# Attention and expert routing on one core: some preparation operations of the first three groups on GpSimd, and a new planned order

## The chip, the core and the metric

The kernel runs on one core of a Trainium2 chip. The metric is the time of one execution on the device in microseconds (us), with inputs and outputs in the chip's memory. Five engines run side by side, each through its own instruction list in order, and wait for one another by semaphores: TensorE (PE; its weight loads are shown as PEld), VectorE (DVE), ScalarE (ACT), GpSimd (POOL) and SyncE (SP, which here only issues transfers). An instruction that must wait holds back everything behind it in its engine's list.

## The reference, cut to what matters

```python
def _attn_ref(q, k, v, g_q, g_k):            # q, k, v: 8 batches, 12 heads, 448 tokens, 64 wide
    def rmsnorm(x, g):
        rms = np.sqrt(np.mean(x * x, axis=-1, keepdims=True) + 1e-06)
        return x / rms * g
    q_n, k_n = (rmsnorm(q, g_q), rmsnorm(k, g_k))
    scores = np.matmul(q_n, k_n.transpose(0, 1, 3, 2)) / np.sqrt(64)
    attn = np.exp(scores - np.max(scores, axis=-1, keepdims=True))
    attn = attn / (np.sum(attn, axis=-1, keepdims=True) + 1e-09)
    return np.matmul(attn, v)

def _moe_ref(x, w_gate, w1, w2):             # x: 3584 tokens, 768 wide; 8 experts, 448 tokens each
    order = np.argsort(-(x @ w_gate).flatten())
    ...                                      # greedy: best pair first, at most 448 tokens an expert
    for e in range(8):
        out[assigned == e] = np.maximum(x[assigned == e] @ w1[e], 0.0) @ w2[e]
```

The attention result, reordered to one row a token, is the input of the routing and of the experts.

## The kernel before, in words

**Three stages.** Attention fills the first 510 us or so of the span. Then the router finds the first expert's tokens, and the eight experts follow, one after another, with the router's later phases woven in between. The change touches attention alone; the experts' code and order are as before.

**How attention is tiled.** The 96 heads are taken in 24 groups of four. A group is two pairs of heads (a = 0 and a = 1 in the code). Queries and keys are prepared per group: ScalarE squares them (`square`), VectorE sums the squares (`sumsq`) and works out the inverse root in six small steps (`rsqrt`, L439 to L449), `norm` (L463) multiplies by it, `gain` (L488) multiplies the queries by the gains. To keep accuracy in float16 each of them is split in a high part (`hi_k`, `hi_q`: ScalarE casts, L493 and L498) and a low part (`lo_k` L525, `lo_q` L530: what the cast lost, a subtraction). High and low parts stand side by side in tiles `ks` and `qs` and are then transposed.

**From there to the output.** `max_score` (L657, L660) multiplies once for the row maxima, `max_reduce` (L671, VectorE) takes the maxima from the accumulation tiles `pm` and `psc`, `put_max` (L675) writes them to the tile `qm`, and they return as one more row of the query operand `q2`. `scores` (L688, L693) then makes the scores in `psc`, ScalarE exponentiates them (`exp`, L704, tile `e`), VectorE or GpSimd makes a low part of some of these (`split`, L720, tile `pl`), and `av` (L739 to L748) multiplies with the values into the accumulation tile `po`. ScalarE and VectorE prepare the values as well (`v_hi` L609, `v_lo` L612, `v_full` L626, `v_tail` L479).

**The first two groups** (g below `EARLY = 2`) are done a pair at a time, so that TensorE has work sooner, and are turned on TensorE (`turn_first`, L552) instead of by transfers. The copies out of that turn are one on VectorE (L558) and one on ScalarE (L564). Their row maxima return through a small TensorE product (`rows_first`, L571) and two copies (L578 on ScalarE, L580 on VectorE). From group 2 on, transposes and row copies are transfers in SP's list: L537 and L507 for `k` and `q`, L587 (`mt<-qm`) and L594 (`q<-mt`) for the row maxima, L801 and L803 (`xt<-xb`, `xt<-xm`) for the attention output of a finished batch (three groups) on its way to the router.

**Which engine does what.** `ENG` gives the engine of each such operation: D is VectorE, P GpSimd, A ScalarE, S a transfer. `FIRST` overrides it for the first groups. Rings limit how far work may run ahead: there is one buffer each for `kn` and `qn`, two for the raw loads (`raw`), three for `k1` and `k2`, two for `q2`.

**What sets the order.** The kernel writes out the whole order of attention itself. `plan` lists some thousands of tasks, each with a queue, an estimated duration (`US`), what it waits for and what it frees. Its place is a number worked out from the group or tile and an offset from the table `P`. `Plan.order` runs through time with a list of free engines and takes, on each engine, the ready task with the lowest place. That sequence is then issued as it stands, on every engine. So a change of one estimate, one engine or one number in `P` can change the order of all the rest. The chip does not see the plan's times, only its order.

**Router work inside attention.** `Router.early` (L1308 to L1348) ranks the experts for the first 21 columns of tokens. It is one task of the plan and gives twelve VectorE instructions in a row.

Of the kernel before, what the change touches and what calls it, by code (L numbers as in the profile page):

```python
# [32 lines left out]
OP = mybir.AluOpType  # L33
# [201 lines left out]
class Attention:  # L235
# [215 lines left out]
    def norm(self, g, i, a=None):  # L451
        name = ("qn", "kn")[i]
# [3 lines left out]
        if g < self.EARLY and i == 0:  # L456
            x = o
        r = self.stat(g, 1, a)[:, i]
        if a is None:
            r = r.rearrange("p (a u) -> p a u", a=2)[:, :, :, None]  # L460
        else:
            r = r[:, :, None]
        self.tt("norm" + "qk"[i], g)(o, x, r.to_broadcast(list(o.shape)), op=OP.mult)  # L463

    ENG = dict(lok="P", loq="P", dupk="S", dupq="S", normk="P", normq="P", gain="P", vfull="A", vtail="A")
    FIRST = (dict(gain="P", normq="P", normk="D", lok="D", loq="D"),
             dict(gain="P", normq="P", normk="P", lok="D", loq="P"), dict(gain="D"))
    TAIL = {}

    def engine(self, e, g):  # L470
        some = self.FIRST[g] if g < len(self.FIRST) else self.TAIL if g >= self.NG - 2 else {}
        return some.get(e, self.ENG[e])

    def tt(self, e, g):
        return (self.nc.gpsimd if self.engine(e, g) == "P" else self.nc.vector).tensor_tensor

# [6 lines left out]
    def gain(self, g, a=None):  # L483
        if g < self.EARLY and not a:
            self.T["qn", g] = self.w.tile([128, 14, 64], F32, name="qn", bufs=self.RINGS["qn"])
        t = self.T["qn", g][:, self.of(a)]
        x = self.raw(g, 0, a) if g < self.EARLY else t
        self.tt("gain", g)(t, x, self.gg[:, None, :].to_broadcast(list(t.shape)), op=OP.mult)  # L488

# [33 lines left out]
    def lo_k(self, g, a=None):  # L523
        t = self.T["ks1", g]
        self.tt("lok", g)(self.half(t, 0, a), self.paired(self.T["kn", g][:, self.of(a)], a), self.half(t, 64, a),  # L525
                          op=OP.subtract)

    def lo_q(self, g, a=None):
        t = self.T["qs1", g]
        self.tt("loq", g)(self.half(t, 64, a), self.paired(self.T["qn", g][:, self.of(a)], a), self.half(t, 0, a),  # L530
                          op=OP.subtract)
# [364 lines left out]
    def gate_sum(self, b):  # L896
# [4 lines left out]

    P = dict(av0=-0.67, av1=-0.55, av3=-233.82, dupk=-20.94, dupq=0.73, early=56.02, exp=-49.79, f01=-18.78,
             f01i=-213.71, f10=-7.45, f10i=-218.14, f11=-6.2, f11i=-725.64, gain=8.07, gate=10.58, gates=0.21,
             gg=-28.49, glast=151.09, gtail=-10.06, hik=40.19, hiq=51.14, lgg=-5.96, lok=10.05, loq=10.17,
             lqk=90.96, lqki=2.37, lqkr=-18.25, ltail=33.72, lv=-4.27, lvs=108.43, lwg=495.86, max=5.38,
             max01=0.85, max10=-25.87, max11=-265.16, ng0=-55.37, ng1=-1.86, normk=5.07, normq=-20, put=-26.68,
             r1=27.99, r2=-773.05, r3=2.11, r4=-73.44, r5=-759.09, r6=46.33, red=-406.74, rows=-84.95, split=-0.52,
             sq0=53.5, sq1=-491.03, ss0=153.72, ss1=175.4, t0=-496.84, t1=3, t2=-38.87, tg6=-1.43, trk1=-75.39,
             trm=-0.91, trq1=7.59, txt=-21.19, vfull=-20.55, vhi=14.06, vlo=44.07, vtail=-509.19, wg=60.43,
             xl=-22.58, xn=58.85, xn1=-39.78, xn2=0.1, xs=-173.13, xst=404.87, xstep=-91.79, xtd=-270.51,  # L910
             xturn=69.89)

# [216 lines left out]
    def plan_first(self, plan, g, a, t):  # L1129
# [11 lines left out]
        raw = [[("raw", 0, i, r) for r in (3 * a, 1, 2)] if g == 0 else [("raw", g, i)] for i in range(2)]  # L1141
        e = lambda name: self.engine(name, g)
        us = lambda name: {"D": d, "P": 0.95}[e(name)]
# [906 lines left out]
```

## Time and profile before

| | us |
|---|---|
| three runs | 1033.56, 1038.93, 1039.92 |
| median | 1038.93 |
| the profiled execution: its own time | 1024.11 |
| the profiled execution: span from first to last instruction | 1022.3 |

The profile shows one execution. Its own time is 1.8 us more than its span, and 14.8 us below the median of the three runs, so a sum that is made against its rows is a difference to be put on the median. Views give start and duration of an instruction in us, the engine, the line, the operation, the tiles as output<-inputs, the shapes, and in square brackets how long the engine sat idle before it and what released it. In a windows view each row is a stretch of time: its length, the busy time and the number of instructions of PE, PEld, DVE, ACT and POOL, the granted TensorE clock as a share of full speed, the transfer engines' share and GB/s.

### The profile page before, as it was taken

Reading aid. Unit: us, or ns where it says so; the run is one execution under the profiler, and the core shown is the slowest. Engines: PE = TensorE matmul, PEld = TensorE weight load, DVE = VectorE, ACT = ScalarE, POOL = GpSimd, SP = SyncE. Lnnn points to the kernel's source line nnn. Section 1 sums busy time; section 2 is a strip of 40 time slices with the busy share of each in tenths; the row PEclk is TensorE's granted clock in tenths of the full one; section 3 lists DMA queues with packets and bytes.
Section 4 is the critical chain, followed back from the end, with each engine's and each line's share of the span. In section 5 each row is a group of like instructions: output and inputs, shape, how many; then the busy total and the mean of one; then the engine's idle time right before and its main releaser. Section 6 shows DMA issues by size and latency. Waiting matters only on the chain. (4 is left out here: it accounts for less than half of the span.)

```text
span 1022.3 us, 23367 instructions
## 1 busy us (share of the span) xinstructions
PE 937.5 (92%) x9495; PEld 598.9 (59%) x9496; DVE 714.3 (70%) x1602; ACT 494.9 (48%) x816; POOL 403.9 (40%) x315
## 2 busy tenths in 40 slices
PE   2698999899898899989969999899999999999996
PEld 1366667667676576656746655555556565555554
DVE  7898878788688778898678777667676866425010
ACT  4767767577676757745514342333342423334111
POOL 3568686687577679653310110101111102020101
PEclk9999999899899999989959999999999999999998
DMA  5268798988879798766137463939493939654101
GB/s 148 70 141 195 151 221 173 184 203 178 199 167 202 181 227 203 146 157 115 45 120 236 158 198 122 265 107 288 134 247 110 300 103 229 234 137 150 39 3 52
DMA packets 275876, 167.01 MB, mean 163 GB/s; under 512 B 195896, under 2 KB 262968, under 8 KB 274744
## 3 DMA queue, kind: packets, MB, share of 16 engines
q1 hardware_dynamic: 251320, 138.70, 56.0%
q0 software_dynamic: 4608, 22.02, 6.4%
q10 hardware_dynamic: 19840, 4.79, 2.2%
q8 instruction: 74, 1.21, 0.5%
q14 instruction: 34, 0.28, 0.1%
HBM read 94.49 MB, written 22.02 MB: 114 GB/s over the span
## 5 line engine op out<-in xcount | busy, mean ns | idle before, releaser
L1835 PE MATMUL ph<-xt,w1h 128*128 128x448 f16 (+2 forms) x804 | 211.2, 344 | 0.8 <-ACT xt L1792 0.5
L739 PE MATMUL po<-v,e 128*128 128x65 f32 (+1 forms) x1392 | 185.8, 270 | 2.0 <-ACT e L704 1.9
L704 ACT ACTIVATE e<-psc 128x896 f32<-128x896 f32 x168 | 152.2, 917 | 65.1 <-PE psc L693 46.6
L739 PEld LDWEIGHTS po<-v,e 128*128 128x128 f32 (+1 forms) x1392 | 157.7, 181 | 28.2 <-issue 20.6
L1868 POOL DMA_INDIRECT out_dram<-y,idx x32 | 32.5, 1014 | 341.5 <-ACT y L1854 266.9
L693 PE MATMUL psc<-q,k 128*128 128x448 f16 x576 | 140.4, 364 | 24.9 <-DVE mx L671 10.2
L720 POOL TENSOR_TENSOR pl<-e 128x896 f16<-128x896 f32 x69 | 119.7, 1734 | 77.9 <-ACT e L704 60.0
L1835 PE MATMUL ph<-xt,w1l 128*128 128x448 f16 (+2 forms) x402 | 136.8, 344 | 0.0
L671 DVE TENSOR_REDUCE mx<-pm 128x2 f32<-128x896 f32 x96 | 104.5, 1088 | 38.1 <-PE pm L660 28.5
L1852 PE MATMUL py<-w2h,hl 128*128 128x384 f16 x384 | 125.5, 327 | 0.2 <-DVE hl L1827 0.2
L1852 PE MATMUL py<-w2h,hh 128*128 128x384 f16 x384 | 125.5, 327 | 0.2 <-ACT hh L1825 0.2
L1852 PE MATMUL py<-w2l,hh 128*128 128x384 f16 x384 | 125.5, 327 | 0.0
L1835 PEld LDWEIGHTS <-w1h 128*128 128x128 f16 x804 | 74.1, 97 | 61.9 <-issue 1.5
L1825 ACT ACTIVATE hh<-ph 128x448 f16<-128x448 f32 x64 | 34.7, 543 | 142.3 <-PE ph L1835 138.7
L744 PEld LDWEIGHTS <-e 128*128 128x128 bf16 (+1 forms) x840 | 88.1, 118 | 22.7 <-issue 18.0
L1852 PEld LDWEIGHTS <-hh 128*128 128x128 f16 x768 | 73.1, 97 | 45.8 <-ACT hh L1825 0.5
L1827 DVE SCALAR_TENSOR_TENSOR hl<-ph,hh 128x448 f16<-128x448 f32 x64 | 39.4, 621 | 78.2 <-ACT hh L1825 78.2
L1854 ACT ACTIVATE y<-py 128x384 f32<-128x384 f32 x48 | 23.5, 490 | 129.3 <-PE py L1852 102.7
L693 PEld LDWEIGHTS <-k 128*128 128x128 f16 x576 | 48.2, 99 | 63.1 <-issue 32.2
L671 DVE TENSOR_REDUCE mx<-psc 128x2 f32<-128x896 f32 x74 | 78.2, 1056 | 0.0
L746 PEld LDWEIGHTS <-e 128*128 128x128 bf16 (+1 forms) x840 | 73.0, 102 | 3.6 <-issue 0.4
L748 PEld LDWEIGHTS <-pl 128*128 128x128 f16 (+1 forms) x840 | 73.4, 102 | 2.1 <-POOL pl L720 2.0
(278 smaller groups left out, 2053.9 us busy)
## 6 DMA issues: line engine op xcount, KB each, us to landing
stage<-in_moe_w_dram SPq DMA_DIRECT2D x64, 768.0 KB
vraw<-in_v_dram SPq DMA_DIRECT2D x24, 384.0 KB
xd<-xb SPq DMA_DIRECT2D x8, 1152.0 KB
qkraw<-in_q_dram SPq DMA_DIRECT2D x23, 384.0 KB
qkraw<-in_k_dram SPq DMA_DIRECT2D x23, 384.0 KB
k<-k SPq DMA_DIRECT2D x44, 112.0 KB
q<-q SPq DMA_DIRECT2D x44, 112.0 KB
xd<-xm SPq DMA_DIRECT2D x16, 96.0 KB
```

The costliest lines, as they stand in the source:

```text
L671: self.nc.vector.tensor_reduce(m, p[:, :k, :448], axis=AX.X, op=OP.max)
L693: nc.tensor.matmul(p[:, i, :448], kt[:, a, 128 * u:128 * u + 128], qt[:, a, 448 * s:448 * s + 448], start=st, stop=not st)
L704: self.nc.scalar.activation(e, p[:, :, :448], AF.Exp, scale=scale)
L720: eng.tensor_tensor(l, self.T["e", d], self.T["ph", d], op=OP.subtract)
L739: nc.tensor.matmul(out, self.T["e", d][:, i, q0:q0 + m], self.v32[g % 2][:, self.by_group(self.WIDE, g).index(d % 7), i, :], start=first, ...
L744: nc.tensor.matmul(out, h[:, i, q0:q0 + m], vh, start=first, stop=False)
L746: nc.tensor.matmul(out[:, :64], h[:, i, q0:q0 + m], vl[:, :64], start=False, stop=False)
L748: nc.tensor.matmul(out, l[:, i, q0:q0 + m], vh, start=False, stop=last)
L1825: nc.scalar.activation(hh, whole, AF.Relu)
L1827: self.later(0.6, lambda: nc.vector.scalar_tensor_tensor(hl, whole, 0.0, hh, op0=OP.max, op1=OP.subtract), k, 3.5, f)
L1835: nc.tensor.matmul(p, a, b[:, o], start=st, stop=sp)
L1852: nc.tensor.matmul(p, a[:, f, s], b[:, f, o], start=st, stop=sp)
```

## The change

Three things are done. `engine` and `tt` take the pair (`a`) as well, so that `FIRST` may name an engine for the second pair alone (`normk1`, `lok1`, `loq1`). Six operations of the first three groups go from VectorE to GpSimd: for group 0 the key norm and both low parts of the second pair, for group 1 the low part of the keys of both pairs, for group 2 the gain. And the table `P` has new numbers throughout, with which the plan gives a new order for the whole of attention.

```diff
-        self.tt("norm" + "qk"[i], g)(o, x, r.to_broadcast(list(o.shape)), op=OP.mult)
+        self.tt("norm" + "qk"[i], g, a)(o, x, r.to_broadcast(list(o.shape)), op=OP.mult)
...
-    FIRST = (dict(gain="P", normq="P", normk="D", lok="D", loq="D"),
-             dict(gain="P", normq="P", normk="P", lok="D", loq="P"), dict(gain="D"))
+    FIRST = (dict(gain="P", normq="P", normk="D", normk1="P", lok="D", lok1="P", loq="D", loq1="P"),
+             dict(gain="P", normq="P", normk="P", lok="P", loq="P"), dict())
...
-    def engine(self, e, g):
+    def engine(self, e, g, a=None):
         some = self.FIRST[g] if g < len(self.FIRST) else self.TAIL if g >= self.NG - 2 else {}
-        return some.get(e, self.ENG[e])
+        return some.get(f"{e}{a}", some.get(e, self.ENG[e]))
-    def tt(self, e, g):
-        return (self.nc.gpsimd if self.engine(e, g) == "P" else self.nc.vector).tensor_tensor
+    def tt(self, e, g, a=None):
+        return (self.nc.gpsimd if self.engine(e, g, a) == "P" else self.nc.vector).tensor_tensor
...
-    P = dict(av0=-0.67, av1=-0.55, av3=-233.82, dupk=-20.94, dupq=0.73, early=56.02, exp=-49.79, f01=-18.78,
...
+    P = dict(av0=0.62, av1=0.31, av3=-126.01, dupk=10.5, dupq=47.72, early=36.44, exp=-2.33, f01=-137.03, f01i=7,
...
-        e = lambda name: self.engine(name, g)
+        e = lambda name: self.engine(name, g, a)
```

`gain`, `lo_k` and `lo_q` pass the pair on in the same way. The new file has one line less ahead of the planned part, so its line numbers from L911 on are one lower.

In the pieces of order below a row is the line, the operation and the tiles with their numbers; the numbers grow along the planned order, so they tell the distance between rows of different engines too. `qn_209`, `kn_248` and `kn_244` are group 0, `st_188` is its statistics, `st_228` those of group 1.

GpSimd near the start, from the query norm of group 0's first pair on; before:

```order
L463 TENSOR_TENSOR qn_209<-qn_209,st_188 128x448
L1210 IOTA tok_89 128x3
L1210 IOTA tok_89 64x1 x2
L1210 IOTA tok_89 128x3
L463 TENSOR_TENSOR qn_209<-qn_209,st_188 128x448
L488 TENSOR_TENSOR qn_337<-qkraw_197,gg_119 128x448 x2
L463 TENSOR_TENSOR qn_337<-qn_337,st_228 128x448 x2
L463 TENSOR_TENSOR kn_411<-qkraw_197,st_228 128x448 x2
L530 TENSOR_TENSOR qs1_413<-qn_337,qs1_413 128x7x64 x2
L720 TENSOR_TENSOR pl_467<-e_432 128x896
```

The same stretch of GpSimd's list now, from the second pair of group 0 on:

```order
L463 TENSOR_TENSOR kn_244<-qkraw_141,st_188 128x448
L463 TENSOR_TENSOR qn_209<-qn_209,st_188 128x448
L525 TENSOR_TENSOR ks1_248<-kn_244,ks1_248 128x7x64
L530 TENSOR_TENSOR qs1_241<-qn_209,qs1_241 128x7x64
L488 TENSOR_TENSOR qn_349<-qkraw_197,gg_119 128x448 x2
L463 TENSOR_TENSOR qn_349<-qn_349,st_228 128x448
L463 TENSOR_TENSOR kn_402<-qkraw_197,st_228 128x448
L530 TENSOR_TENSOR qs1_409<-qn_349,qs1_409 128x7x64
L525 TENSOR_TENSOR ks1_421<-kn_402,ks1_421 128x7x64
L463 TENSOR_TENSOR qn_349<-qn_349,st_228 128x448
L463 TENSOR_TENSOR kn_402<-qkraw_197,st_228 128x448
L530 TENSOR_TENSOR qs1_409<-qn_349,qs1_409 128x7x64
```

The norm of the keys and the two low parts of group 0's second pair stand in GpSimd's list now, and group 1 goes through it a pair at a time.

ScalarE between the squares of group 1 and the high parts of group 0's second pair; before (`po_257` and `po_273` are the turned queries and keys of group 0's first pair):

```order
L419 ACTIVATE sq_253<-qkraw_197 128x448 x2
L564 ACTIVATE q2_0_125<-po_257 64x896
L441 ACTIVATE st_228<-st_228 128x2x7
L443 ACTIVATE st_228<-st_228 128x2x7
L441 ACTIVATE st_228<-st_228 128x2x7
L564 ACTIVATE k2_0_122<-po_273 64x896
L443 ACTIVATE st_228<-st_228 128x2x7
L498 ACTIVATE qs1_241<-qn_209 128x7x64
```

And now (`po_259` and `po_276` are the same two):

```order
L419 ACTIVATE sq_255<-qkraw_197 128x448 x2
L609 ACTIVATE vs_0_131<-vraw_0_129 128x10x64
L564 ACTIVATE q2_0_125<-po_259 64x896
L441 ACTIVATE st_228<-st_228 128x2x7
L626 ACTIVATE v32_0_135<-vraw_0_129 128x2x64 x5
L564 ACTIVATE k2_0_122<-po_276 64x896
L443 ACTIVATE st_228<-st_228 128x2x7
L441 ACTIVATE st_228<-st_228 128x2x7
L479 ACTIVATE vt_0_133<-vs_0_131 64x260 x2
L443 ACTIVATE st_228<-st_228 128x2x7
L493 ACTIVATE ks1_248<-kn_244 128x7x64
```

The work on the values of group 0 has moved ahead of the copy of the first keys, and ahead of the second pair's high parts.

VectorE ahead of the twelve instructions of `Router.early`, near the end of attention; before (`mx_6483` are the maxima of group 21, `st_6200` the statistics of group 23, the last one):

```order
L671 TENSOR_REDUCE mx_6483<-pm_6641 128x2
L899 TENSOR_TENSOR logits_63<-po_6579,lsc_6658 128x24
L900 TENSOR_TENSOR logits_63<-po_6579,lsc_6658 64x8
L675 TENSOR_SCALAR qm_1_128<-mx_6483 128x14
L449 SCALAR_TENSOR_TENSOR st_6200<-st_6200 128x28
L1308 TENSOR_REDUCE best_98<-logits_63 128x21
```

And now, first ahead of the twelve and then around their end (`mx_6458` are the maxima of group 21, `st_6271` the statistics of group 23):

```order
L449 SCALAR_TENSOR_TENSOR st_6271<-st_6271 128x28
L671 TENSOR_REDUCE mx_6458<-psc_6523 128x2
L771 TENSOR_SCALAR z_6610<-po_6472 128x7
L773 RECIPROCAL z_6610<-z_6610 128x7
L775 TENSOR_TENSOR po_6472<-po_6472,z_6610 128x7x64
L671 TENSOR_REDUCE mx_6458<-pm_6604 128x2
L671 TENSOR_REDUCE mx_6458<-psc_6607 128x2
L792 TENSOR_TENSOR xb_6345<-po_6472,xb_6345 128x2x3x64
L793 TENSOR_TENSOR xm_6346<-po_6472,xm_6346 128x64
L899 TENSOR_TENSOR logits_63<-po_6549,lsc_6658 128x24
L900 TENSOR_TENSOR logits_63<-po_6549,lsc_6658 64x8
L671 TENSOR_REDUCE mx_6458<-pm_6664 128x2
```

```order
L1316 CAST key_102<-keyi_101 128x21
L1317 TENSOR_SCALAR key_102<-keyi_101 128x21
L1347 TENSOR_TENSOR cmp_103<-key_102,hit0_76 128x672
L675 TENSOR_SCALAR qm_1_128<-mx_6458 128x14
L771 TENSOR_SCALAR z_6835<-po_6684 128x7
L671 TENSOR_REDUCE mx_6837<-pm_6775 128x2
```

The last group's statistics are ready twelve rows ahead of the router's block instead of right before it, and `put_max` of group 21 stands behind the block instead of ahead of it. In GpSimd's list the norms, gain and key low part of the last group (tiles 6564 to 6627) now have lower numbers than the block's surroundings (6664 to 6835), where before they had numbers among and behind them (6705 to 6808).

More of the change, by code (lines that the diff above doesn't have):

```diff
@@ L487, in gain @@
         x = self.raw(g, 0, a) if g < self.EARLY else t
-        self.tt("gain", g)(t, x, self.gg[:, None, :].to_broadcast(list(t.shape)), op=OP.mult)
+        self.tt("gain", g, a)(t, x, self.gg[:, None, :].to_broadcast(list(t.shape)), op=OP.mult)
     def hi_k(self, g, a=None):
@@ L524, in lo_k @@
         t = self.T["ks1", g]
-        self.tt("lok", g)(self.half(t, 0, a), self.paired(self.T["kn", g][:, self.of(a)], a), self.half(t, 64, a),
+        self.tt("lok", g, a)(self.half(t, 0, a), self.paired(self.T["kn", g][:, self.of(a)], a), self.half(t, 64, a),
                           op=OP.subtract)
@@ L529, in lo_q @@
         t = self.T["qs1", g]
-        self.tt("loq", g)(self.half(t, 64, a), self.paired(self.T["qn", g][:, self.of(a)], a), self.half(t, 0, a),
+        self.tt("loq", g, a)(self.half(t, 64, a), self.paired(self.T["qn", g][:, self.of(a)], a), self.half(t, 0, a),
                           op=OP.subtract)
@@ L900, in gate_sum @@
         nc.vector.tensor_tensor(L[h:h + 64, m], p[h:h + 64, 3, :8], sc[h:h + 64, 3], op=OP.add)
-    P = dict(av0=-0.67, av1=-0.55, av3=-233.82, dupk=-20.94, dupq=0.73, early=56.02, exp=-49.79, f01=-18.78,
[L903 to L911, printed above, removed]
+    P = dict(av0=0.62, av1=0.31, av3=-126.01, dupk=10.5, dupq=47.72, early=36.44, exp=-2.33, f01=-137.03, f01i=7,
+             f10=-20, f10i=-101.01, f11=-63.88, f11i=-4.25, gain=-17.31, gate=-61.49, gates=611.71, gg=-37.05,
+             glast=531.4, gtail=25.71, hik=-23.33, hiq=-12.46, lgg=-30, lok=-45.64, loq=-19.7, lqk=19.14,
+             lqki=2.33, lqkr=-10.74, ltail=-0.48, lv=39.8, lvs=-0.58, lwg=50, max=5.36, max01=-23.6, max10=-9.43,
+             max11=0, ng0=3.77, ng1=0, normk=-28.56, normq=-35.58, put=-51.1, r1=-19.6, r2=-14.29, r3=-125.45,
+             r4=-13.5, r5=-13.4, r6=-13.3, red=40.8, rows=-4.79, split=-26.06, sq0=11.38, sq1=-12.03, ss0=229.42,
+             ss1=-108.84, t0=36.83, t1=29.52, t2=7.83, tg6=-23.17, trk1=4.92, trm=8.32, trq1=428.26, txt=45.83,
+             vfull=32.86, vhi=43, vlo=419.11, vtail=1.37, wg=88.45, xl=-145.18, xn=0.13, xn1=1.85, xn2=34.71,
+             xs=-74.17, xst=536.22, xstep=-4.52, xtd=27.08, xturn=347.32)
     US = dict(small=0.2, copyA=0.95, vhi=0.74, vlo=0.82, vtailA=0.85, vfullA=0.23, vfullD=0.2, sumsq=1.08, normP=1.69,
```

## The prediction

> **What bounds the kernel now.** I read the engines' busy time over the whole span first, then the same in stretches, then the timeline of each engine where a stretch shows idle time.
>
> ```profile
> PE 937.5 (92%) x9495; PEld 598.9 (59%) x9496; DVE 714.3 (70%) x1602; ACT 494.9 (48%) x816; POOL 403.9 (40%) x315
> ```
>
> ```profile
> 0.00:50.00 50.00, 21.75 (x130) 11.68 (x130) 39.67 (x110) 29.56 (x59) 22.63 (x36) 1.00 0.40 110
> 50.00:500.00 450.00, 417.55 (x5210) 294.36 (x5208) 370.32 (x602) 300.40 (x546) 311.92 (x174) 0.97 0.82 175
> 500.00:550.00 50.00, 38.49 (x688) 27.99 (x686) 38.13 (x136) 12.99 (x22) 7.21 (x15) 0.73 0.43 136
> 550.00:1022.00 472.00, 459.76 (x3478) 264.88 (x3475) 266.19 (x757) 151.96 (x192) 62.12 (x91) 0.99 0.54 161
> ```
>
> TensorE is the bound: 92% of the span. Its work is not changed, so time can only come from its idle stretches and from its clock. The last stretch, the experts, keeps its order. In the third the router's chain runs, which has its old order too. What the change can touch is the first 50 us, with 28.3 us of idle TensorE, and the 450 us behind them, with 32.5 us idle and a clock of 0.97, which costs up to 3% of 450 = 13.5 us more.
>
> In the first stretch VectorE is the engine to look at:
>
> ```profile
> 12.00:62.00 50.00, 32.34 (x213) 17.32 (x214) 43.98 (x83) 33.58 (x64) 21.05 (x22) 1.00 0.48 123
> ```
>
> From the first sums to the last row maximum of group 1 it is busy 43.98 of 50 us, GpSimd 21.05. TensorE's rows there show what it waits for:
>
> ```profile
> 19.91 0.90 PE L660 MATMUL pm<-k,q 64*128 64x448 f16 x2 [2.54 <-ACT k L564]
> 32.94 0.93 PE L660 MATMUL pm<-k,q 64*128 64x448 f16 x2
> 50.02 0.55 PE L660 MATMUL pm<-k,q 64*128 64x448 f16 x2
> 51.00 0.93 PE L693 MATMUL psc<-q,k 128*128 128x448 f16 x4
> ```
>
> These are the first maxima of group 0's first pair, of its second pair, of group 1's first pair, and the first scores that need the second pair.
>
> **Term 1, the start: six operations leave VectorE.** Their rows:
>
> ```profile
> 20.59 0.62 DVE L463 TENSOR_TENSOR kn<-qkraw,st 128x448 f32<-128x448 f32 x1
> 23.88 0.62 DVE L530 TENSOR_TENSOR qs<-qn,qs 128x448 f16<-128x448 f32 x1
> 27.35 0.61 DVE L525 TENSOR_TENSOR ks<-kn,ks 128x448 f16<-128x448 f32 x1
> 37.07 1.45 DVE L525 TENSOR_TENSOR ks<-kn,ks 128x448 f16<-128x448 f32 x1
> 38.44 1.66 DVE L439 SCALAR_TENSOR_TENSOR st<-st,eps 128x28 f32<-128x28 f32 x1
> 40.02 0.61 DVE L525 TENSOR_TENSOR ks<-kn,ks 128x448 f16<-128x448 f32 x1
> 48.52 1.78 DVE L488 TENSOR_TENSOR qn<-qn,gg 128x896 f32<-128x896 f32 x1
> ```
>
> All but the row at 38.44 go: 0.62 + 0.62 + 0.61 + 1.45 + 0.61 + 1.78 = 5.7 us. On GpSimd they cost more:
>
> ```profile
> 33.64 1.83 POOL L463 TENSOR_TENSOR kn<-qkraw,st 128x448 f32<-128x448 f32 x2
> 35.43 2.61 POOL L530 TENSOR_TENSOR qs<-qn,qs 128x448 f16<-128x448 f32 x2
> L488 POOL TENSOR_TENSOR qn<-qn,gg 128x896 f32<-128x896 f32 x21 | 43.9, 2093 | 0.0
> ```
>
> One norm at 0.92, four low parts at 1.3 and one gain at 2.09 are 8.2 us. GpSimd's 29 us idle in that window cover them as busy time; what does not vanish is their latency, and that GpSimd works in order.
>
> Followed through the new order with these durations: the work on the values now stands ahead of ScalarE's copy of the first keys.
>
> ```profile
> 18.94 0.91 ACT L564 ACTIVATE k<-po 64x896 f16<-64x896 f16 x1
> 23.95 1.36 ACT L609 ACTIVATE vs<-vraw 128x640 f16<-128x640 f32 x2 [2.14 <-issue]
> 28.30 1.11 ACT L626 ACTIVATE v<-vraw 128x128 f32<-128x128 f32 x5
> ```
>
> Half of 1.36 and all of 1.11 pass it, part of them in 0.77 us in which ScalarE waited, so that copy and the first maxima come about 1.2 us later, at 21.1. The second pair then gains. Its key low part waited for VectorE until 27.35; on GpSimd it runs behind the high part, about 23 to 24.3, and its first maxima start near 31.3 instead of 32.94. The maxima of group 1's first pair, at 50.02 before, now stand ahead of the values product and fall near 41 to 46. By my count the scores that need the second pair can start near 49.5 instead of 51.0, with group 1's first maxima, about 2.2 us of TensorE (four rows like those at 50.02, 0.35 to 0.55 each), already done. 1.5 + 2.2 = 3.7 us; I take 3, since the later statistics of group 1's second pair (GpSimd's norms of it near 40 instead of 32.75) eat some. Bounds: 5.7 gained, if all that leaves VectorE counts; 2 lost, if the 1.2 us stay and the order on GpSimd delays group 1.
>
> Against the gain speaks the row at 38.44: a step on a 28-wide tile took 1.66 us while GpSimd ran the two low parts at 35.43 and then a split; the same step elsewhere took 0.17:
>
> ```profile
> 18.48 0.17 DVE L439 SCALAR_TENSOR_TENSOR st<-st,eps 128x14 f32<-128x14 f32 x1
> ```
>
> So a moved operation can hold VectorE up for about its own length. [...]
>
> **Term 2, the router's block at 439 us.** Twelve VectorE instructions run in a row while GpSimd is never idle:
>
> ```profile
> 438.89 1.79 DVE L1309 TENSOR_TENSOR score<-logits,best 128x168 bf16<-128x168 f32 x1
> 440.60 1.60 DVE L1313 TENSOR_SCALAR keyi<-best 128x21 int32<-128x21 int32 x1
> 449.50 0.84 DVE L1348 TENSOR_TENSOR cmp<-key,hit 128x672 bf16<-128x672 f32 x1
> 512.30 0.16 DVE L1313 TENSOR_SCALAR keyi<-best 128x7 int32<-128x7 int32 x1
> 438.80:450.40 11.60, 10.68 (x140) 8.62 (x140) 11.54 (x13) 6.18 (x7) 11.60 (x7) 1.00 0.66 197
> ```
>
> The block took 11.5 us. GpSimd runs seven instructions there, and nearly each holds up one step by some 1.5 us (1.60 against 0.16). Behind it TensorE stands, and its clock falls:
>
> ```profile
> 452.52 0.92 PE L693 MATMUL psc<-q,k 128*128 128x448 f16 x4 [3.04 <-DVE mx L671]
> 457.04 2.40 PE L693 MATMUL psc<-q,k 128*128 128x448 f16 x6 [1.77 <-ACT e L704]
> 450.00:460.00 10.00, 5.71 (x28) 2.58 (x27) 9.13 (x15) 3.15 (x8) 3.72 (x2) 0.70 0.46 97
> ```
>
> This episode costs 4.3 us idle and 30% of 10 us in clock, 7.3 us. In the new order the last group's statistics are ready twelve rows ahead of the block, so GpSimd has done most of that group's preparation by then; by their numbers four of its instructions remain beside the block, not seven. Three hold-ups of 1.5 us less are 4.5 us. But the row maximum of group 21 now leaves behind the block, and its way back as a row starts that much later. I take 2 us. Bounds: 7.3 gained, if the episode vanishes; 4 lost, if that row comes 2 us late and the clock falls once more (about 2 us).
>
> **All else that moves** is the order of the other 400 us. The number of instructions in each stage is the same, so I cost it at nothing, under cover of a TensorE that is 93% busy there; if that cover is gone, it shows as more episodes like this one:
>
> ```profile
> 254.85 3.51 SPq L801 DMA_TRANSPOSE xt<-xb  x2
> 258.46 1.62 SPq L594 DMA_DIRECT2D q<-mt  x2
> 263.01 1.30 PE L693 MATMUL psc<-q,k 128*128 128x448 f16 x3 [2.75 <-DMA q<-mt]
> 180.00:200.00 20.00, 17.60 (x170) 11.99 (x166) 14.85 (x23) 11.56 (x22) 12.51 (x8) 0.83 0.99 189
> 260.00:270.00 10.00, 7.25 (x38) 3.87 (x38) 5.11 (x8) 3.61 (x4) 5.55 (x3) 0.66 0.99 212
> 350.00:360.00 10.00, 8.61 (x91) 5.75 (x91) 8.56 (x16) 8.22 (x20) 3.17 (x2) 0.83 0.50 116
> ```
>
> The row maxima of a group were issued behind two transposes of the attention output, TensorE waited, and the clock fell: 2.75 idle and 34% of 10 us, about 6 us. With the one at 452 the windows show four episodes in which the clock falls, of 3 to 7 us each.
>
> **The sum.** 3 + 2 = 5 us less than the profiled execution's 1024.1, so 1019.1 there. The three runs have a median of 1038.93, 14.8 us above it; the difference is put on that: 1034.
>
> **The rivals.** First, nothing arrives (about 1039): GpSimd's 8.2 us more hold VectorE up for as long as it was relieved, or both terms are lost in later waits. For it speaks the row at 38.44; against it, that half of VectorE's 43.98 us there are reductions, L671 and L431:
>
> ```profile
> 12.00:62.00 50.00, 14.68 (x16) 1.00 0.48 123
> 12.00:62.00 50.00, 8.60 (x11) 1.00 0.48 123
> ```
>
> They took their usual 1.1 us a full tile beside GpSimd as well (14.68 and 8.60 us for 16 and 11 of them, half tiles among them).
>
> Second, slower: in the new order the row maxima are issued closer to the scores that need them. Measured in tile numbers, the distance from a group's row transpose to its first exponentials falls from a mean of 206 to 188, and at groups 2, 16 and 21 to 134, 136 and 153. Each group that comes too late costs an episode of about 6 us as at 263. One cancels the forecast; from two on it decides: 1038.9 - 5 + 12 = 1046. Against it: the group that waited at 263 has 202, a usual distance, so the distance alone does not decide.
>
> Third, much faster: two of the four episodes go as well as the start's 3 us. 1038.9 - 3 - 12 = 1024. For it: the new order has been drawn for the whole stage. Against it: nothing in it removes the transposes that stand ahead of the row copies.
>
> A new order also shifts when TensorE reaches full speed at the start. The pair of rows at 32.94 and 50.02, 0.93 against 0.55 for the same two products, shows that this happened between them. [...]
>
> **How the numbers follow.** Forecast (gain of 1 to 9 us, 1030 to 1038): 0.40. Nothing arrives (1038 to 1042): 0.20. More late row maxima (1042 to 1051): 0.22. Much faster (1020 to 1030): 0.18. A change of 1%, 10.4 us, is about what a measurement here can tell from none: below 1028.5 lies most of the last case, 0.16, and a little of the first, 0.03, so faster 0.19; above 1049.3 lies nearly half of the third, 0.10; within 1% 0.71. The range 1024 to 1047 leaves out about 0.1 at each end: two episodes fewer, or two more.
>
> **What would show it.** Right: the first maxima near 21, the second pair's near 31 and those of group 1 well ahead of 50; the block of L1307 to L1347 in 6 to 9 us, and no idle of 3 us behind it. Wrong: VectorE steps of 1.6 us in the first 50 us in greater number; a wait of TensorE's scores for `q<-mt` at more places than one; a clock below 0.97 from 50 to 500 us. The forecast falls if those stretches differ by more than 5 us in either direction with the start as foreseen.

## The result, and the profile after

| | before | after |
|---|---|---|
| executions side by side | 20 | 20 |
| median, us | 1033.16 | 1042.71 |
| lowest and highest, us | 1028.34 to 1040.2 | 1030.22 to 1055.8 |
| span of the profiled execution, us | 1022.3 | 1043.1 |

The ratio of after to before is 1.0064, with a 95% interval of 1.0039 to 1.0090: the change makes the kernel slower by about 7 us. The ratio leaves out executions that lie more than 1.5% above the fastest of their kernel, which is why it is smaller than the quotient of the medians, 1.0092. The two profiled executions lie further apart than the kernels do: 1044.85 against 1024.11 us, where the means of the twenty are 1042.5 and 1033.7. So the profiles show where time is lost, and more of it than an average execution loses.

The windows view of after, by the same stages as before (length, busy time and count of PE, PEld, DVE, ACT and POOL, granted clock, transfer share, GB/s):

```profile
0.00:50.00 50.00, 24.83 (x154) 12.38 (x155) 39.23 (x112) 31.09 (x61) 27.05 (x41) 0.97 0.42 113
50.00:500.00 450.00, 420.09 (x4817) 295.55 (x4818) 340.21 (x568) 285.22 (x518) 302.97 (x172) 0.91 0.80 172
500.00:550.00 50.00, 38.22 (x838) 29.04 (x835) 37.78 (x92) 20.63 (x39) 12.72 (x12) 0.84 0.19 59
550.00:1043.00 493.00, 477.88 (x3698) 277.39 (x3695) 285.42 (x827) 158.61 (x198) 66.74 (x98) 0.98 0.56 165
```

The second row has the loss. TensorE is no more idle there than before (29.9 us against 32.5), but its clock is 0.91 instead of 0.97, and with the same busy time it gets through 4817 recorded instructions instead of 5210. The lost clock is worth 0.06 of 450 us, 27 us.

The start came as foreseen. TensorE's rows in after: first maxima of group 0's first pair, of its second pair, of group 1, and the first scores that need the second pair.

```profile
21.14 0.90 PE L660 MATMUL pm<-k,q 64*128 64x448 f16 x2 [3.62 <-ACT k L564]
30.06 0.92 PE L660 MATMUL pm<-k,q 64*128 64x448 f16 x2 [1.54 <-DVE q L558]
38.08 0.55 PE L660 MATMUL pm<-k,q 64*128 64x448 f16 x2 [0.86 <-DVE mx L671]
49.05 0.93 PE L693 MATMUL psc<-q,k 128*128 128x448 f16 x4 [0.87 <-DVE q L580]
```

So did the router's block: VectorE's rows from its first to its last instruction, and then TensorE's last wait ahead of its end and the first behind it.

```profile
461.82 0.33 DVE L1307 TENSOR_REDUCE best<-logits 128x21 f32<-128x168 f32 x1
462.19 2.15 DVE L1308 TENSOR_TENSOR score<-logits,best 128x168 bf16<-128x168 f32 x1
464.26 0.16 DVE L1312 TENSOR_SCALAR keyi<-best 128x21 int32<-128x21 int32 x1
465.60 0.85 DVE L1347 TENSOR_TENSOR cmp<-key,hit 128x672 bf16<-128x672 f32 x1
```

```profile
459.77 1.65 PE L693 MATMUL psc<-q,k 128*128 128x448 f16 x4 [0.53 <-ACT e L704]
488.13 0.92 PE L693 MATMUL psc<-q,k 128*128 128x448 f16 x4 [0.51 <-ACT e L704]
```

The block takes 4.6 us instead of 11.5, with one hold-up instead of six, and the wait of 3.04 us behind it is gone. What neither part explains is what happens from 340 to 425 us: ScalarE's 106th exponential, the first of group 15, still starts 2.9 us earlier than before (341.3 against 344.2), the 127th, the first of group 18, 21.7 us later (420.3 against 398.6). Among the stretches with the clock at half three are long, here as windows of their own:

```profile
80.50:94.00 13.50, 12.24 (x78) 8.26 (x77) 10.07 (x15) 4.43 (x7) 8.90 (x5) 0.50 0.74 185
340.00:363.50 23.50, 23.50 (x180) 18.19 (x179) 8.16 (x16) 10.41 (x20) 11.68 (x7) 0.50 0.36 90
408.50:421.50 13.00, 12.15 (x99) 8.88 (x98) 6.22 (x13) 5.82 (x12) 7.22 (x4) 0.50 0.75 185
```

That is 50 us at 0.50, worth 25 us of work at full clock, and TensorE is shown as busy in 47.9 of them: it is not waiting there, it is slow. TensorE's timeline around the longest one:

```profile
336.00 0.36 PE L660 MATMUL pm<-k,q 64*128 64x448 f16 x2 [0.78 <-DVE mx L671]
336.99 0.92 PE L693 MATMUL psc<-q,k 128*128 128x448 f16 x4 [0.35 <-DVE mx L671]
339.62 0.87 PE L693 MATMUL psc<-q,k 128*128 128x448 f16 x2 [1.71 <-DVE mx L671]
340.42 0.96 PE L688 MATMUL psc<-q,k 128*64 128x448 f16 x4
341.30 1.12 PE L739 MATMUL po<-v,e 128*128 128x65 f32 x4
...
353.04 1.68 PE L693 MATMUL psc<-q,k 128*128 128x448 f16 x4
...
359.03 1.09 PE L739 MATMUL po<-v,e 128*128 128x65 f32 x4
...
360.10 3.18 PE L693 MATMUL psc<-q,k 128*128 128x448 f16 x8
...
363.25 0.79 PE L739 MATMUL po<-v,e 128*128 128x65 f32 x4
```

There is a stall of some 3 us in pieces (0.25 us at 334.85 belongs to it), and then 20 us in which nearly all is values products, 65 columns wide; only four scores products (353.04) and eight for row maxima stand among them. The first long run of 448-column products is that at 360.10, and with it the clock comes back: the same four values products take 1.09 us at 359.03 and 0.79 at 363.25. The other two stretches are alike. A stall stands at the head of each:

```profile
81.76 0.56 PE L660 MATMUL pm<-k,q 64*128 64x448 f16 x2 [3.95 <-DVE mx L671]
409.35 0.21 PE L744 MATMUL po<-vt,e 128*128 128x65 f16 x1 [2.62 <-ACT vt L479]
```

Both run into values products, and end with scores (at 91.18 and 418.62 us). Before had stalls too: its TensorE waited for 1 us or more 11 times between 50 and 500 us, and after's also 11 times. But behind before's stall at 263 us scores came within 7 us (3.25 us of L693 alone, beside 2.19 us of L739's values products), and the clock was back after 6.8 us:

```profile
267.23 0.94 PE L693 MATMUL psc<-q,k 128*128 128x448 f16 x2
268.98 1.22 PE L693 MATMUL psc<-q,k 128*128 128x448 f16 x4
```

This gives a theory, *stall, then values products*: a stall of some 3 us halves the clock; wide products bring it back within a few us, values products alone don't; and the new order puts values products behind its stalls. The rivals: the moved operations themselves cost (*engines*); the executions differ by chance (*chance*); TensorE has nothing else in its list at those places, so work moved there would remove the stall (*empty list*); and the scores come late whatever the clock does (*late rows*).

### The profile page after: what moved, and what is told of

It reads as the page before. It is cut to its first block, busy times and chain, and to the rows that moved or that the text cites. A ratio compares the mean times of both kernels' runs of the same rounds, so it can differ in the third digit from the quotient of the medians.

```text
span 1043.1 us, 23345 instructions
## 1 busy us (share of the span) xinstructions
PE 961.0 (92%) x9495; PEld 614.4 (59%) x9496; DVE 702.6 (67%) x1596; ACT 495.6 (48%) x816; POOL 409.5 (39%) x321
## 5 line engine op out<-in xcount | busy, mean ns | idle before, releaser
L739 PE MATMUL po<-v,e 128*128 128x65 f32 (+1 forms) x1392 | 199.6, 286 | 0.5 <-DVE q L558 0.5
L739 PEld LDWEIGHTS po<-v,e 128*128 128x128 f32 (+1 forms) x1392 | 167.7, 194 | 27.2 <-issue 21.2
L693 PE MATMUL psc<-q,k 128*128 128x448 f16 x576 | 146.7, 378 | 16.6 <-ACT e L704 8.7
L1834 PEld LDWEIGHTS <-w1h 128*128 128x128 f16 x804 | 74.2, 97 | 62.1 <-issue 1.5
L744 PEld LDWEIGHTS <-e 128*128 128x128 bf16 (+1 forms) x840 | 91.7, 124 | 19.7 <-issue 13.5
L693 PEld LDWEIGHTS <-k 128*128 128x128 f16 x576 | 49.0, 101 | 58.5 <-issue 33.3
L746 PEld LDWEIGHTS <-e 128*128 128x128 bf16 (+1 forms) x840 | 75.5, 106 | 9.1 <-issue 5.2
L748 PEld LDWEIGHTS <-pl 128*128 128x128 f16 (+1 forms) x840 | 75.5, 105 | 4.4 <-POOL pl L720 2.9
```

Source lines behind the costliest of these rows:

```text
L693: nc.tensor.matmul(p[:, i, :448], kt[:, a, 128 * u:128 * u + 128], qt[:, a, 448 * s:448 * s + 448], start=st, stop=not st)
L739: nc.tensor.matmul(out, self.T["e", d][:, i, q0:q0 + m], self.v32[g % 2][:, self.by_group(self.WIDE, g).index(d % 7), i, :], start=first, ...
L744: nc.tensor.matmul(out, h[:, i, q0:q0 + m], vh, start=first, stop=False)
L746: nc.tensor.matmul(out[:, :64], h[:, i, q0:q0 + m], vl[:, :64], start=False, stop=False)
L748: nc.tensor.matmul(out, l[:, i, q0:q0 + m], vh, start=False, stop=last)
L1834: nc.tensor.matmul(p, a, b[:, o], start=st, stop=sp)
```

## The experiments

In the tables a time is the median of a kernel's executions in its series, the clock is the mean of their granted clocks; three single executions above 1200 us (1717 and 5002 of before, 3747 of the kernel with its stalls filled) are left out of that mean. The medians of before in the four series were 1031.74, 1030.16, 1034.74 and 1033.07 us.

### The two halves of the change, and both kernels again

The engine at issue is taken from a table of its own, so that the planned order and the engines can be set apart. Engines alone: the order of before, with the six operations issued on GpSimd. Order alone: the order of after, with them on VectorE.

```diff
     def tt(self, e, g, a=None):
-        return (self.nc.gpsimd if self.engine(e, g, a) == "P" else self.nc.vector).tensor_tensor
+        x = self.ISSUE[g] if g < len(self.ISSUE) else self.TAIL if g >= self.NG - 2 else {}
+        return (self.nc.gpsimd if x.get(f"{e}{a}", x.get(e, self.ENG[e])) == "P" else self.nc.vector).tensor_tensor
```

> The order of before on every engine, with the six operations issued on GpSimd at the places that they have in it (on VectorE they are simply gone). Theory 'order' (the loss is from the new planned order, the six operations cost nothing or help): 1030 to 1034 us, 0.997 to 1.001 of before, the granted clock from 50 to 500 us at 0.96 or more. Theory 'engines' (GpSimd beside VectorE holds VectorE up, so the moved operations themselves cost): 1036 to 1044 us, 1.003 to 1.010, with VectorE steps of 1.6 us in greater number in the first 60 us. Theory 'chance' (the order differs little, where the clock falls differs by execution): 0.998 to 1.002.

> The order of after, with the six operations issued on VectorE as before. Theory 'order': 1040 to 1050 us, 1.005 to 1.015 of before (the order's loss of 6 us, and up to 5 us of the start's gain given back), the clock from 50 to 500 us at 0.94 or less. Theory 'engines': 0.998 to 1.003. Theory 'chance': 0.998 to 1.005, the clock's falls at other places than in the profile of after.

> Before unchanged, for a second profile and the noise: 0.998 to 1.002. Theory 'order': the clock from 50 to 500 us at 0.96 or more again, its falls near 190, 263 and 452 us again. Theory 'chance': falls at other places, and a clock that may as well be 0.91.

> After unchanged, for a second profile: 1.003 to 1.010 of before. Theory 'order': the clock from 50 to 500 us at 0.94 or less again, with falls near 85, 345 and 415 us again. Theory 'chance': a clock of 0.95 to 0.98 there in this execution, the falls at other places, and the fall of 20 us at 340 us not there.

| kernel | executions | us | clock | ratio to before |
|---|---|---|---|---|
| engines alone | 12 | 1034.34 | 0.958 | 0.9954 (0.9907 to 1.0001) |
| order alone | 6 | 1043.74 | 0.948 | 1.0108 (1.0064 to 1.0153) |
| before again | 12 | 1031.23 | 0.962 | 0.9998 (0.9970 to 1.0026) |
| after again | 12 | 1042.15 | 0.952 | 1.0058 (1.0017 to 1.0099) |

The order costs about 11 us and the engines cost nothing; whether they gain is not settled, since their interval ends at 1 and their median is 2.6 us above that of before. The theory *engines* falls. The theory *chance* falls as well: the second profile of after has the same three long stretches, 0.5 to 4 us later,

```profile
81.00:94.50 13.50, 12.09 (x76) 8.27 (x77) 10.22 (x15) 4.59 (x7) 9.06 (x5) 0.50 0.76 181
344.00:366.50 22.50, 22.50 (x175) 17.54 (x174) 8.24 (x16) 9.90 (x19) 11.05 (x6) 0.50 0.37 91
412.50:425.50 13.00, 13.00 (x104) 9.02 (x103) 7.55 (x18) 5.02 (x11) 7.22 (x4) 0.50 0.80 182
```

and the order alone has them at 83, 342.5 and 407 us, each 12.5 to 13.5 us long. Chance stays in the single execution: after ran between 1030 us at a clock of 0.962 and 1055 at 0.932 in this series. Before again had its falls at 187, 266 and 457 us, as expected, and four others of 3.4 to 6.8 us elsewhere; the clock of engines alone from 50 to 500 us was 0.95, a little below the 0.96 expected. The loss goes with the clock: after's mean lies 8.6 us above before's (1040.5 against 1031.9) and its clock 0.008 below, which is about 8 us of 1030.

Where the time goes in the single profiles, by the start of ScalarE's exponentials (the four are the first of groups 1, 15, 18 and 23; each trace has all 168):

| exponential | before | after | after again | engines alone | order alone |
|---|---|---|---|---|---|
| 8th | 65.1 | 59.9 | 60.6 | 62.1 | 62.6 |
| 106th | 344.2 | 341.3 | 345.4 | 345.7 | 343.7 |
| 127th | 398.6 | 420.3 | 423.0 | 404.7 | 414.1 |
| 162nd | 492.6 | 515.1 | 517.0 | 499.6 | 506.8 |

The start's gain of about 5 us in after is there (3.0 us by the profile of the engines alone, 2.5 by that of the order alone), and is lost at 80 to 94 us. From the 106th to the 127th before takes 54.4 us, engines alone 59.0, order alone 70.4, and after 79.0 and 77.6.

### More work behind the stall

```diff
-        for i in self.turns(d):
+        for i in self.turns(d) * (4 if d == 106 else 1):
```

> After, with the six score products of task 106, the first ones behind the wait at 339.62, done four times over (18 more products, 448 columns wide, the first three rounds overwritten; the output is unchanged). Theory 'values products keep the clock low' (the half clock of 340 to 363.6 us lasts as long as TensorE runs 65-wide values products alone, and ends with the first stretch of 448-wide products that fills a few us, as it did with the scores at 360.10): the clock is back at 1.00 by 349 us instead of 363.6, although TensorE has 3.7 to 5.5 us more to do; the 127th exponential comes 2 to 6 us earlier than the 423 to 424.5 of the two profiles of after. Rival 'set time' (the half clock after such a stall lasts some 22 us whatever runs): the clock at 0.50 until 363 us or later, and the 127th exponential 3 to 6 us later than 424.

```profile
339.05 2.05 PE L693 MATMUL psc<-q,k 128*128 128x448 f16 x5 [1.23 <-DMA q<-mt]
341.03 0.96 PE L688 MATMUL psc<-q,k 128*64 128x448 f16 x4
341.92 0.80 PE L693 MATMUL psc<-q,k 128*128 128x448 f16 x2
342.65 0.57 PE L688 MATMUL psc<-q,k 128*64 128x448 f16 x4
```

The stall was there, the clock fell at 339 us, and it was back at 342.5: four L688 products take 0.96 us at 341.03 and 0.57 at 342.65. Half clock lasted 3.4 us instead of 24, and the 127th exponential came at 412.1 instead of 420.3 and 423.0, with more work done. The rival of a set time falls; so it does by the order alone, where the same stall was followed by 13.7 us at half clock. That spread, and that this is one profile, make the size of the gain uncertain. As a whole this kernel was not shown to be faster than after (four executions, 1041.4 us, ratio 1.0117, 1.0044 to 1.0190).

### Moving work into the stalls

One group: the preparations of the values of group 14 and six of its values products go ahead, to where TensorE stalls at 336 us. Three stalls: this, and similar moves at 77 us (VectorE) and 404 us (ScalarE). Each pair says what is put behind what in the planned order.

```diff
+    MOVES = ((('v_hi', 14), ('exp', 99)), (('v_lo', 14), ('put_max', 15)), (('v_full', 14), ('exp', 101)),
+             (('v_tail', 14), ('square', 18, 0)), (('av', 196), ('max_scores', 114)), (('av', 199), ('av', 196)),
...
+             (('max_scores', 23), ('av', 20)), (('max_reduce', 23), ('put_max', 2)),
...
+             (('v_tail', 17), ('x_hi', 33)), (('load_qk', 22, 1), ('rsqrt', 21, 3)),
```

> The order of after, with the four preparations of the values of group 14 (L609, L612, L626, L479) moved up ahead of the row maxima of group 16 on ScalarE and VectorE, and six of its values products moved up between those row maxima on TensorE; nothing else moves. Theory 'empty list' (TensorE stalls at 334 to 340 us because its list holds only row maxima and scores there, with the values products that could have filled the gap behind them): the 3 us of idle time between 334 and 340 go, the clock stays at 0.95 or more from 330 to 370, the 127th exponential comes 8 to 15 us earlier than at 424, and the time is 0.992 to 1.000 of before. Rival 'late rows' (the scores of group 16 wait for their row maxima anyway): the stall reappears ahead of those scores, the clock falls there, and the time stays at 1.003 to 1.010.

> As the one-group kernel, and two more local moves in the order of after: at 77 us the row maxima tasks 23 and 24 ahead of the sums' steps and the values' low part on VectorE; at 404 us the loads issued from ScalarE's list (L377) behind the exponential and the values' tail that they held up, with the low part and tail of group 17 moved up. Theory 'empty list': the clock from 50 to 500 us at 0.95 or more instead of 0.91, and 0.983 to 0.993 of before. Rival 'late rows': 0.998 to 1.008, with new falls of the clock near the same groups.

| kernel | executions | us | clock | ratio to before |
|---|---|---|---|---|
| one group | 11 | 1042.09 | 0.948 | 1.0131 (1.0093 to 1.0170) |
| three stalls | 12 | 1038.12 | 0.953 | 1.0067 (1.0029 to 1.0104) |

Both expectations of *empty list* missed. TensorE's rows of the one-group kernel, in which lines stand 20 higher, and of the one with three stalls (30 higher):

```profile
332.91 0.92 PE L713 MATMUL psc<-q,k 128*128 128x448 f16 x4 [2.04 <-ACT e L724]
352.65 0.38 PE L677 MATMUL pm<-k,q 64*64 64x448 f16 x4 [2.14 <-DVE mx L691]
```

```profile
327.46 1.65 PE L723 MATMUL psc<-q,k 128*128 128x448 f16 x4 [2.03 <-ACT e L734]
348.83 0.59 PE L687 MATMUL pm<-k,q 64*64 64x448 f16 x4 [4.09 <-DVE mx L701]
```

The stall at 336 to 340 us went, and two others took its place, one ahead of it, for ScalarE's exponentials, and one behind it, for VectorE's maxima. In its one profile the one-group kernel has 10.2 us at half clock there instead of 24, and its 127th exponential at 412.3, but its eleven executions are no faster than after. What they lose elsewhere I can't say. In both kernels, filling a stall with work that was due soon only moved it. As to the waits behind, *late rows* holds; the wait ahead it did not foresee.

### Filling the stalls with products that are not needed

The same three stalls of after, filled with 39 products of 448 columns into the accumulation tile of the next values products, which overwrite it. The control has as many products where TensorE does not wait.

```diff
+    FILL = {('max', 25): (3, 3, 16), ('max', 116): (28, 15, 3), ('scores', 106): (28, 15, 8), ('av', 238): (34, 18, 12)}
+    def fill(self, what, n):
+        pair, g, times = self.FILL.get((what, n), (0, 0, 0))
...
+        for _ in range(times):
+            p = self.T["po", pair].rearrange("p a b -> p (a b)")[:, :448]
+            self.nc.tensor.matmul(p, self.T["k1", g][:, 0, :128], self.T["q1", g][:, 0, :448], start=True, stop=True)
```

> After, with 39 products of 448 columns added on TensorE inside the three stalls that precede its long half-clock stretches: 16 ahead of the row maxima 25 (81.76 us), 12 in pieces of 3, 1 and 8 ahead of row maxima 116 and scores 106 (336 to 339.6), 12 ahead of the values product 238 (409); they write to accumulation space that the next values products overwrite, so the output is unchanged, and nothing else moves. Theory 'stall, then values products' (a stall of some 3 us halves the clock, and the values products behind it keep it there for 14 to 24 us): the clock does not fall at these three places, the low stretches from 50 to 500 us come to less than 55 us instead of 89 to 90, the mean clock of the runs rises from 0.951 to 0.960 or more, and the time falls by 6 to 15 us against after, to 0.993 to 1.002 of before, although work was added. Rival 'late rows' (the time is lost in waits, the clock only follows): the waits move behind the added products, 1.005 to 1.012. Rival 'chance': the clock falls elsewhere as often, 1.003 to 1.010.

> Control: after with the same 39 products added where TensorE does not wait (16 ahead of scores 24, 11 ahead of scores 92, 12 ahead of scores 115). Theory 'stall, then values products': nothing gained, 39 products of 0.2 us cost up to 8 us, 1.006 to 1.016 of before, the long low stretches near 81, 340 and 409 us still there. If dense work anywhere raises the clock: as fast as the kernel with the products in the stalls.

| kernel | executions | us | clock | ratio to before |
|---|---|---|---|---|
| stalls filled | 12 | 1031.15 | 0.966 | 0.9954 (0.9915 to 0.9993) |
| same work elsewhere | 12 | 1044.77 | 0.952 | 1.0075 (1.0028 to 1.0122) |

The fill (L652) in TensorE's timeline at the three places, and then the windows of the same three stretches as above:

```profile
79.14 3.20 PE L652 MATMUL po<-q,k 128*128 128x448 f16 x16
...
339.35 1.68 PE L652 MATMUL po<-q,k 128*128 128x448 f16 x8
...
396.43 2.43 PE L652 MATMUL po<-q,k 128*128 128x448 f16 x12
```

```profile
79.00:92.00 13.00, 11.07 (x105) 6.98 (x102) 12.90 (x20) 5.10 (x10) 8.96 (x6) 1.00 0.70 168
339.00:362.00 23.00, 22.68 (x280) 16.54 (x279) 16.50 (x30) 15.38 (x28) 15.92 (x9) 1.00 0.64 150
396.00:409.00 13.00, 13.00 (x181) 9.22 (x179) 10.22 (x19) 7.63 (x15) 7.95 (x6) 1.00 0.99 192
```

The clock does not fall at any of them, and TensorE gets through 280 instructions in 23 us where it did 180. The 127th exponential comes at 406.2 us. The kernel is 1.0% faster than after (0.9954 against 1.0058 and 1.0064) with 39 products more, and it is now below before. In the control the stalls and the long stretches stay (13.7, 17.1 and 10.2 us), and nothing is gained:

```profile
82.72 0.56 PE L660 MATMUL pm<-k,q 64*128 64x448 f16 x2 [3.97 <-DVE mx L671]
407.77 0.19 PE L748 MATMUL po<-vt,e 128*128 128x65 f16 x1 [3.05 <-ACT vt L479]
```

This settles where the loss came from: the three stalls, by way of the clock. Products that nobody needs can't shorten a wait, and the same ones elsewhere gained nothing.

### The router's block, and two faster versions

Block later: engines alone, with the router's twelve instructions moved down behind `x_lo` of pair 40. Block later and fill: in addition the first half of scores 77 and 119 is repeated while the second half waits for the row maxima. Fill more: after with the three stalls filled, and the first half of scores 63 and 77 repeated.

```diff
+    MOVES = ((('early',), ('x_lo', 40)),)
...
+    AGAIN = {77: 11, 119: 8}
...
+                for _ in range(self.AGAIN.get(d, 0) if st and i == self.turns(d)[0] else 0):
+                    nc.tensor.matmul(p[:, i, :448], kt[:, a, :128], qt[:, a, :448], start=True, stop=True)
```

> The engines-alone kernel (order of before) with the router's twelve VectorE instructions moved down, behind the last group's preparation on GpSimd. Theory of the prediction's second term (GpSimd's instructions hold the block up by 1.5 us each, and the block holds up the row maxima behind it): the block takes 4 to 6.5 us instead of 11.5, the wait of 3.04 us behind it goes, and the time is 2 to 7 us less than the engines-alone kernel's, 0.988 to 0.994 of before. Rival (the cover holds: TensorE would wait there for something else): the block is shorter, but the time is the same as the engines-alone kernel's, 0.994 to 0.998.

> The kernel with the block moved down (order of before, engines of after), with the first half of scores 77 and 119 repeated 11 and 8 times while their second half waits for the row maxima (2.7 to 3.0 us waits behind q<-mt at 275 and 401 us). Theory 'stall, then values products': the falls at 276 and 402 us go or get shorter, 2 to 6 us less than that kernel, 0.988 to 0.994 of before, the mean clock 0.966 to 0.972. Rival: the fill only replaces idle time, the clock falls as often: 0.994 to 0.999.

> The kernel with the three stalls filled, and besides the first half of scores 63 and 77 repeated 5 and 10 times while their second half waits for the row maxima (1.46 us at 225 and 2.57 us at 264 in its profile). Theory 'stall, then values products': the fall of 7 us at 265 goes; a half clock of 7 us costs 3.5 us, so 1 to 4 us less than the kernel with three stalls filled, 0.991 to 0.995 of before, the mean clock of the runs 0.966 to 0.971. If the repeated products delay the second halves: 0.996 to 1.000.

| kernel | executions | us | clock | ratio to before |
|---|---|---|---|---|
| block later | 12 | 1026.33 | 0.964 | 0.9951 (0.9917 to 0.9986) |
| block later and fill | 12 | 1025.98 | 0.969 | 0.9928 (0.9894 to 0.9961) |
| fill more | 12 | 1025.64 | 0.973 | 0.9933 (0.9885 to 0.9980) |

The block took 4 us at its later place, but the wait came along; it is there in the profile of block later and fill too (3.09 us at 469.38). VectorE's first and last row of the block, and TensorE's wait behind it (lines 11 higher):

```profile
479.19 0.32 DVE L1319 TENSOR_REDUCE best<-logits 128x21 f32<-128x168 f32 x1
482.32 0.85 DVE L1359 TENSOR_TENSOR cmp<-key,hit 128x672 bf16<-128x672 f32 x1
```

```profile
485.23 0.59 PE L668 MATMUL pm<-k,q 64*64 64x448 f16 x4 [3.10 <-DVE mx L682]
```

By ratio this is the engines-alone kernel (0.9951 against 0.9954), which is what the rival said; by medians it is 8 us less, of which 1.6 lie between the two series. I leave open whether the shorter block is worth anything. The fills fit their expectations by time and mean clock, but what they add is not shown: the interval of block later and fill overlaps that of block later, and so does that of fill more with the stalls filled. In the one profile of block later and fill the falls at 276 and 402 us are gone, and two others of 10 and 14 us stand at 218 and 324. With the two more in after, one stretch of half clock is left between 50 and 500 us (10.2 us), the window's clock is 0.99, and the clock of all executions is the highest of any kernel here. Both versions are about 0.7% faster than before and 1.3% faster than after.

## Why the prediction was wrong

**Term 1 was right.** It had 21.1, 31.3, 41 to 46 and 49.5 us for the four rows at the start, which stand at 21.14, 30.06, 38.08 and 49.05, the third 3 us earlier than foreseen. It took 3 us; the 8th exponential comes 4.5 to 5.2 us earlier in the two profiles of after, within its bounds. What it left out has the size of the rest: full clock came to stay at 42.7 and 43.4 us in the two profiles of after, and at 47.7 and 47.6 in those of before. At half clock 4 to 5 us longer cost some 2 us, an estimate. The first rival, that GpSimd would hold VectorE up for as long as it was relieved, falls by the engines-alone kernel: the six operations on GpSimd cost nothing. VectorE's rows of after from 30 to 60 us have no step of 1.6 us; the longest of its small steps there is one of 0.95 us at 31.62 (L447, which took 0.17 at 29.40 in before). The long steps are there elsewhere, put there by the order: 2.15 us at 462.19, and `put_max` right ahead of the first long stall, while GpSimd ran a gain from 75.60 on:

```profile
76.00 1.72 DVE L675 TENSOR_SCALAR qm<-mx 128x14 f16<-128x14 f32 x1
```

It took 1.71 and 1.73 us in after again and order alone, and 0.18 in before and engines alone. VectorE has no idle time from there to the maxima that TensorE waits for at 81.76, so some 1.5 of those 3.95 us are this one step.

**Term 2 was right in its rows and not shown in its gain.** The block took 4.6 us, below the 6 to 9 foreseen, and the idle time behind it went from 3.04 to 0.51 us. But the clock was at half from 459 to 469 us all the same, from a fall ahead of the block, and in the block-later kernel the wait of 3 us only moved.

**The step that failed was the third: "All else that moves is the order of the other 400 us … so I cost it at nothing".** The cover it named, a TensorE that is 93% busy there, was kept: idle time (29.9 us against 32.5) and the number of waits of 1 us or more (11 and 11) did not rise. What changed is what stands behind the waits in TensorE's list, and with that how long the clock stays low: 23.9 us behind the stall at 340 us, and 3.4 us behind the same stall with 18 wide products more. The order alone costs about 11 us. Without the three long stretches after's profile has 34 us at half clock in six pieces, no more than before's second profile.

**The second rival had the right sign, and two of three places.** It named groups 2, 16 and 21; the losses are ahead of groups 2 and 16, and at group 18. Its mechanism was only near: TensorE did not wait for the row transfer there (all its waits for `q<-mt` from 50 to 500 us come to 3.3 us, against 4.4 before) but for VectorE's maxima and for the values' tail. Its price was too small. I took 6 us an episode from those of before, whose half clock lasted 3.4 to 6.8 us; the three new ones last 13.7 to 23.9 us, 7 to 12 us each. By the price of before, three of them would have been 18 us; by their own length they are 25. I gave this rival 0.22 against 0.40 for the forecast, because the order was judged by distances of row maxima and not by what TensorE runs while the clock is low. That the measured 1042.7 us falls into the bracket of this rival, and into the range of 1024 to 1047, is partly luck: all of them were counted from the three runs' 1038.93, 5.8 us above the median of twenty. As a difference, the kernel lost 7 to 10 us where a gain of 5 was forecast.

**The third rival**, faster by fewer falls, went the other way: 9 low stretches from 50 to 500 us, 85 us long together, against 4 and 24 us in before's profile and 7 and 34 in its second one.

## What to carry to other kernels

When a new order leaves the busy and idle times as they were, look at the granted clock in short windows next, and at what TensorE runs behind each stall: here a stall of 2.75 us, with wide products soon behind it, cost some 3 us of clock (6.8 us at half), and stalls of 2.6 to 4.0 us with narrow ones behind them cost 7 to 12 (13.7 to 23.9 us at half). A stall that can't be removed can be filled with products that nobody needs, if there is accumulation space that will be overwritten anyway; 39 of them in the three stalls were worth 1% here. Work that is due soon was a worse filling here, since the stall reappeared.

## What the runs showed of the hardware that was not expected

- TensorE shown as busy throughout did not bring the clock back. From 341.3 to 360.1 us, nearly all of it values products (65 columns, with a weight load each, weight loads shown in 16.4 of the 18.8 us), it stayed at 0.50, and half clock ended behind 3.2 us of 448-column products. In the kernel with more scores, with 448-column products alone behind the same stall, half clock lasted 3.4 us. Whether the difference goes with the width, the weight loads or the float32 products was not tried.
- The clock fell without one long idle time. Ahead of 340 us the longest wait was 1.71 us, and the waits come to 3.1 us in four pieces. TensorE was busy for 1.34 of the 3.40 us ahead of the fall:

```profile
336.30:339.70 3.40, 1.34 (x9) 0.63 (x7) 3.06 (x7) 0.95 (x6) 0.25 (x1) 1.00 0.96 206
```

- The clock changes in steps. In each of the 14 profiles all its changes behind 50 us lie on one grid of 3.41 us, which lies differently in each execution; after's nine low stretches are 4, 2, 1, 2, 1, 7, 1, 4 and 3 steps long. Cut into these steps, from 60 to 500 us, the profiles show what precedes a fall: of the steps at full clock with TensorE busy for less than half all 36 were followed by one, of those from 0.5 to 0.7 41 of 108, of those from 0.7 to 0.86 5 of 175, and of those above none of 1291; in the profiles of before and after alone 6 of 6, 6 of 14, 1 of 23 and none of 180. So the length of one wait does not decide: in after waits of 1.50, 1.56 and 1.13 us, with none longer near them, were followed by half clock at 193, 316 and 384 us. And of the steps at half clock with TensorE busy for over 98%, none of the 48 with less than 0.7 of a scores product in it brought full clock back (in before and after none of the 10 with at most 0.31 us of scores products).
- Within one series after's mean clock went from 0.932, in an execution of 1055 us, to 0.962 in one of 1030. Half clock was not seen behind every wait of one length either: in before's profile it followed one of 1.49 us that ended at 182.70, and not one of 1.52 us that ended at 411.22. What decides this was not tried. A single profile is a poor measure of an order.
